# More unread products on TensorE, one ring slot more and one fewer, and fewer pooled sums on VectorE

## The chip, the cores and the metric

The kernel runs on one core of a Trainium2 chip. The metric is the time of one execution on the device, in microseconds. A core has five engines that run their own instruction queues in order: TensorE (PE in the profile; its weight loads are PEld), VectorE (DVE), ScalarE (ACT), GpSimd (POOL) and SyncE (SP), which issues most of the transfers.

## The reference

Three stages in a chain, all in float32, for 4 batches of 576 tokens:

```python
# 1 attention, 8 heads of 64: pooled by 4, plus a local window
q_d, k_d, v_d = (a.reshape(B, H, S // 4, 4, D).mean(axis=3) for a in (q, k, v))
x = np.repeat(sm_attn(q_d, k_d, v_d), 4, axis=2)        # softmax attention over 144 keys
x = x + local_attn(q, k, v)                             # keys with |i - j| < 4
# 2 experts: 8 of them, 512 -> 1024 -> 512, one per token
fresh_e = argmax(x @ w_gate)
e = fresh_e if s == 0 or sigmoid(x @ w_local) < 0.5 else prev_e   # prev_e of token s - 1
x = p[e] * (relu(x @ w1[e]) @ w2[e])                    # p: softmax of the gate
# 3 mixer
u = x + (relu(x.T @ w_tok1) @ w_tok2).T                 # over 576 tokens, hidden 256
out = u + relu(u @ w_ch1) @ w_ch2                       # 512 -> 1536 -> 512
```

## The kernel before

The work is split over a few classes. `Attn` does the attention and the routing, batch by batch. `Early` computes two of the experts, 256 rows each, for tokens of the first three batches, still inside the attention program. `Lead` fetches the first weights and rows of the rest. `Moe` then runs all experts by rank, and its `overflow` is a loop, with a length known only at run time, over surplus rows. `Mix` is the mixer. A float32 product is done as three products of high and low parts (the names wh, wl and c2h, c2l are such parts).

Three recorded programs follow one another: attention with `Early` and `Lead`, then `Moe`, then `Mix`. Class `Sched` records each operation with an estimated duration, and `Sched.order` puts the operations of a program into one order by simulating the engines, the buffers and priorities; line 527, 529 or 531 is where recorded operations are issued, so nearly all rows of the profile carry these lines. Each engine then executes its own operations in that order, and an operation that waits holds up everything behind it on its engine.

Buffers are rings. In attention `kz` (5 slots) holds the keys of a pair of heads, `vw` (NVW = 4 slots) values, `raw` (NRAW = 3 slots) loads that POOL sums up; a slot has 4 KB or more per partition. `Early` takes its weights through the same rings: `raw` for what SP loads, `kz` for the high parts and `vw` for the low parts.

Keys are pooled by four in `pool_k`, for each batch b, pair of heads pr (0 to 2) and half u, either by one sum on VectorE or by three additions on POOL:

```python
if (b, u) in KDVE:
    i("dve", "tensor_reduce", out=kd, in_=kv, axis=AX.X, op=ALU.add)
else:
    for k in range(1, 4):
        i("pool", "tensor_tensor", out=kd, in0=kd if k > 1 else kv[:, :, :, 0], in1=kv[:, :, :, k], op=ALU.add)
```

KDVE lists five pairs (b, u), so 15 of the 24 sums are on VectorE. Values of the batches 1 to 3 are pooled by POOL (`vd`, from `raw`). POOL also divides the local softmax (`p`) and builds masks for routing (`r_dg`).

`Sched.warm` adds products that nobody reads (lhsT `onesb`, rhs `rb`, 128x248, bf16; "unread products" below). After the planning it walks along TensorE's planned times, and where a planned gap has room it adds one, as long as the planned busy time of the last WINDOW = 3.4 us is below a share of it:

```python
used = sum(max(0.0, min(e, t) - max(b, t - WINDOW)) for b, e in done[-60:])
if cold or used < share * WINDOW:
    new.append((t, fn))
```

In the attention program (line 1694) the share is WARM = 0.5; in `Mix` (line 1667) MIX_WARM = (10.0, 0.5), that is the first 10 planned us with a share of 0.5. `Moe` has none. Between the programs of `Moe` and `Mix` stands the loop of `overflow`: line 1459 reads its length, and at line 1460 all engines meet before it (rows of semaphores at that line). Behind it, `Mix` begins with gathers on POOL (`x_f<-yd,pos`), then PE's transposes `x_t` of the rows.

Of the kernel before, what the change touches and what calls it, by code (L numbers as in the profile page):

```python
# [219 lines left out]
class Sched:  # L220
# [80 lines left out]
    def i(self, e, m, after=(), **kw):  # L301
        outs = [kw[k] for k in ("out", "accum_out") if kw.get(k) is not None]
        ins = [v for k, v in kw.items() if k not in ("out", "accum_out") and isinstance(v, (bass.AP, View))]
        acc = [(region(a), True) for a in outs] + [(region(a), False) for a in ins]
        c = self.cost(e, m, outs[0], ins, kw)
        if self.cur is not None:
            o = self.ops[self.cur]
            assert o["e"] == e
            o["calls"].append((m, kw))
            o["d"] += c  # L310
        else:
            self.ops.append(dict(e=e, calls=[(m, kw)], d=c, pred={}, use=[], init=None, stage=self.stage + self.shift, moves=True))
        k = len(self.ops) - 1
        o = self.ops[k]
        for p in after:
            o["pred"].setdefault(p, 0)
        for a in outs + ins:
            if isinstance(a, View) and a.buf not in o["use"]:
                o["use"].append(a.buf)
                a.buf.users.append(k)  # L320
        self.note(k, acc)
        return k
# [211 lines left out]
class Attn:  # L534
# [108 lines left out]
    def pool_k(self, b, pr):  # L643
# [5 lines left out]
        for u in range(2):  # L649
            r = slice(64 * u, 64 * u + 64)  # L650
            kv = kz[r, u, :, 3:195].rearrange("p h (g r) -> p h g r", r=4)
            kd = s["kd"][r, :, 48 * pr:48 * pr + 48]
            if (b, u) in KDVE:
                i("dve", "tensor_reduce", out=kd, in_=kv, axis=AX.X, op=ALU.add)
# [266 lines left out]
    def run(self, early):  # L921
        S_ = self.S
        do = lambda name, b, *args: S_.late((name, b), getattr(self, name), b, *args)
        do("load_q", 0)
        self.load_consts()
        for b in range(B):
            t0 = STEP * 3 * b
            S_.stage = t0 - D_LEAD * STEP if b else D0
            if b:
                do("load_q", b)  # L930
            for pr in range(3):
                do("load_u", b, pr)
                do("pool_k", b, pr)
                if pr:
                    do("pool_v", b, pr - 1)
            for hp in range(HP):
                do("pool_q", b, hp)
                do("d1", b, hp)
                do("d2", b, hp)
            for pr in range(3):  # L940
                S_.stage = t0 + STEP * pr
                do("l1", b, pr)
                do("l2", b, pr)
                for n in ((0,), (1, 2), (3, 4))[pr]:
                    do("x1", b, n)
            S_.stage = t0 + 3 * STEP + R_LAG * STEP
            if b == B - 1:
                stage, S_.stage = S_.stage, t0 + E_LAG * STEP
                S_.late("take", self.early.take)
                S_.stage = stage  # L950
            elif b == B - 2:
                S_.stage = t0 + 3 * STEP + E_LAG * STEP
            do("route", b)
            if b == B - 3:
                self.early = early()
# [142 lines left out]
def convert(S_, src, n, hi, lo, after=(), cf="cf", cs="cs", queue="dma"):  # L1098

    i = S_.i  # L1100
    raw = S_.next("cr")
    if src.dtype == mybir.dt.int64:
        i(queue, "dma_start", after=after, out=raw[:, 0:2 * n], in_=src.bitcast(I32))
        rv = raw[:, 0:2 * n].rearrange("p (n t) -> p n t", t=2)
        low, high = rv[:, :, 0], rv[:, :, 1]
        f = S_.next(cf, I32)[:, 0:n]
        i("dve", "tensor_scalar", out=f, in0=high, scalar1=3, scalar2=0x3FFFFFF8, op0=ALU.logical_shift_left, op1=ALU.bitwise_and)
        i("dve", "scalar_tensor_tensor", out=f, in0=low, scalar=29, in1=f, op0=ALU.logical_shift_right, op1=ALU.bitwise_or)
        i("dve", "scalar_tensor_tensor", out=f, in0=high, scalar=-0x40000000, in1=f, op0=ALU.bitwise_and, op1=ALU.bitwise_or)
        sq = S_.next(cs, F32)[:, 0:n]  # L1110
        i("act", "activation", out=sq, in_=high.bitcast(F32), func=AF.Square)
        f = f.bitcast(F32)
        i("pool", "tensor_single_scalar", out=sq, in_=sq, scalar=FLOOR, op=ALU.is_ge)
        i("pool", "tensor_tensor", out=f, in0=f, in1=sq, op=ALU.mult)
    else:
        f = raw.bitcast(F32)[:, 0:n]
        i(queue, "dma_start", after=after, out=f, in_=src)
    i("act", "copy", out=hi, in_=f)
    i("dve", "tensor_tensor", out=lo, in0=f, in1=hi.bitcast(F32), op=ALU.subtract)
# [252 lines left out]
class Moe(Experts):  # L1372
# [54 lines left out]
    def run(self):  # L1427
        NW = KF * NE
        prev, done = None, []
        t0 = 0.0  # L1430
        for n in range(NW):
            r, fb = divmod(n, KF)
            self.S.stage = t0
            t0 += 4 * (12 * CAPS[r] / 2400 + TILES[r] * 0.65)
            if n >= NLEAD:
                self.loadw(n)
            if fb == 3 and r + 1 < NE:
                self.gather(r + 1)
            h = self.mm1(r, fb)
            if prev is not None:  # L1440
                self.mm2(*prev)
            prev = (r, fb, h)
            done.append(len(self.S.ops) - 1)
            if n == 24:
                self.S.stage = t0
                self.zeros()
            if n >= 8 and n % CONV == 0 and self.jobs:
                self.S.stage = t0 + 60
                convert(self.S, *self.jobs.pop(0), after=(done[n - 6],))
        self.mm2(*prev)  # L1450
        assert not self.jobs
        self.S.issue(self.S.order(busy=dict(pe=PE_LATE)))

    def overflow(self):
        tc, nc = self.tc, self.nc
# [44 lines left out]
class Mix:  # L1500
# [147 lines left out]
    def run(self):  # L1648
# [18 lines left out]
        filler = lambda: self.nc.tensor.matmul(cold, at.onesb, at.rb, start=True, stop=True)  # L1667
        self.S.issue(self.S.warm(self.S.order(), filler, 0.107, MIX_WARM[0], MIX_WARM[1]))

# [46 lines left out]
            Mix(a, tc, at, rt, yd, out, c1t, c2, c2t, wtt).run()  # L1716


WARM, WINDOW = 0.5, 3.4
NKZ, NVW, NRAW = 5, 4, 3  # L1720
VPE = (0,)
KDVE = ((0, 0), (0, 1), (1, 0), (2, 0), (3, 0))
STEP, D_LEAD, R_LAG = 12.0, 1.0, 1.5
SLACK = 0.02
PE_LATE = 2.0
NLEAD, CONV, C2_EARLY = 1, 2, 4
RAW, RING = 3, 4
RING_F, TOK_FB = 26, 3
MIX_WARM = 10.0, 0.5
MARK = 1, 0  # L1730
SHIFT = {('d1', 0): -8, ('pool_qk', 0): 5, ('load_q', 0): -5, ('x1', 3): 14, ('load_u', 0): 1, ('load_v', 2): 9, ('route', 2): -8, ('load_u', 3): -9, ('d1', 1): 15, ('load_q', 1): 4, ('pool_qk', 3): 10, ('route', 3): 4, ('x1', 0): 5, ('l1', 3): -6, ('l1', 0): -5, ('d2', 2): -1, ('load_k', 3): -2, ('Lead', 'gather'): -8, ('Early', 'gather'): -23, ('load_v', 1): 2}
WARM0 = 0.0
# [23 lines left out]
```

## Time and profile before

| | us |
|---|---|
| median of three executions | 818.44 |
| lowest, highest | 816.65, 822.51 |
| profiled execution | 815.2 |
| its span in the trace | 813.4 |
| TensorE busy | 764.6 (94%) |
| TensorE weight loads | 635.8 (78%) |
| VectorE busy | 464.5 (57%) |
| ScalarE busy | 331.1 (41%) |
| GpSimd busy | 231.5 (28%) |
| mean granted TensorE clock | 0.987 |

Attention with the early experts lasts until about 214 us, the experts until 439 us, the mixer to the end. A share of busy time over the whole span mixes these three; the rows below go by stage. The profile names what ended an engine's idle time behind an arrow (`<-DVE sm` is an operation of VectorE that writes sm). A granted clock of 1.0 is 2.4 GHz on TensorE, 0.50 is 1.2 GHz.

### The profile page before, as it was taken

Reading aid. Unit: us, or ns where it says so; the run is one execution under the profiler, and the core shown is the slowest. Engines: PE = TensorE matmul, PEld = TensorE weight load, DVE = VectorE, ACT = ScalarE, POOL = GpSimd, SP = SyncE. Lnnn points to the kernel's source line nnn. Section 1 sums busy time; section 2 is a strip of 40 time slices with the busy share of each in tenths; the row PEclk is TensorE's granted clock in tenths of the full one; section 3 lists DMA queues with packets and bytes.
Section 4 is the critical chain, followed back from the end, with each engine's and each line's share of the span. In section 5 each row is a group of like instructions: output and inputs, shape, how many; then the busy total and the mean of one; then the engine's idle time right before and its main releaser. Section 6 shows DMA issues by size and latency. Waiting matters only on the chain. (4 is left out here: it accounts for less than half of the span.)

```text
span 813.4 us, 13914 instructions
## 1 busy us (share of the span) xinstructions
PE 764.6 (94%) x5318; PEld 635.8 (78%) x5318; DVE 464.5 (57%) x1025; ACT 331.1 (41%) x722; POOL 231.5 (28%) x191
## 2 busy tenths in 40 slices
PE   7898987978999998999896999999999999999998
PEld 4566774857898887888795887888888888888897
DVE  6688989696557878899952767531441144111121
ACT  1775867534435454666552534311321132110110
POOL 4676414450624546436401165200000000000000
PEclk9899999999999999999999999999999999999999
DMA  9986324636699866878664233002001200010010
GB/s 253 245 231 211 119 99 122 184 129 196 212 299 302 274 223 198 278 225 274 215 200 149 69 100 113 27 27 72 13 1 27 72 14 0 1 52 0 1 52 27
DMA packets 36346, 107.90 MB, mean 133 GB/s; under 512 B 5003, under 2 KB 5643, under 8 KB 35895
## 3 DMA queue, kind: packets, MB, share of 16 engines
q1 hardware_dynamic: 32359, 95.15, 37.2%
q0 software_dynamic: 3200, 10.28, 4.2%
q10 hardware_dynamic: 720, 1.57, 0.5%
q8 instruction: 42, 0.69, 0.3%
q14 instruction: 25, 0.20, 0.1%
HBM read 87.32 MB, written 19.66 MB: 132 GB/s over the span
## 5 line engine op out<-in xcount | busy, mean ns | idle before, releaser
L531 DVE SCALAR_TENSOR_TENSOR x_h<-x_m,x_h 128x512 fp32r<-128x512 f32 (+1 forms) x60 | 38.2, 637 | 194.9 <-ACT x_h L531 194.9
L527 PE MATMUL x_y<-x_h,c2h 128*128 128x512 f32 (+1 forms) x480 | 136.2, 369 | 0.0
L531 ACT ACTIVATE x_h<-x_m 128x512 fp32r<-128x512 f32 (+1 forms) x60 | 33.3, 554 | 201.1 <-PE x_m L527 176.1
L527 PEld LDWEIGHTS x_y<-x_h,c2h 128*128 128x128 f32 x480 | 86.6, 189 | 14.3
L527 PE MATMUL x_y<-x_h,c2l 128*128 128x512 f32 (+1 forms) x240 | 88.3, 368 | 0.0
L527 PE MATMUL y<-wh,h 128*128 128x512 f32 (+2 forms) x205 | 74.8, 402 | 1.8 <-DVE yo L531 1.2
L531 DVE TENSOR_TENSOR wl<-raw,wh 128x1024 fp32r<-128x1024 f32 (+1 forms) x47 | 59.9, 1277 | 18.4 <-ACT wh L531 18.0
L531 ACT CAST wh<-raw 128x1024 fp32r<-128x1024 f32 (+1 forms) x47 | 47.1, 1004 | 21.6 <-PE y L527 15.2
L531 POOL TENSOR_SCALAR cs<-cs 128x512 f32<-128x512 f32 (+1 forms) x21 | 38.1, 1812 | 49.8 <-ACT cs L531 49.1
L527 PEld LDWEIGHTS x_y<-x_h,c2l 128*128 128x128 f32 x240 | 45.2, 189 | 7.6
L527 PEld LDWEIGHTS y<-wh,h 128*128 128x128 f32 (+2 forms) x205 | 38.2, 188 | 12.1 <-DVE yo L531 2.5
L531 POOL TENSOR_TENSOR cf<-cf,cs 128x512 f32<-128x512 f32 (+1 forms) x21 | 39.6, 1884 | 27.9 <-DVE cf L531 26.3
L527 PE MATMUL y<-wl,h 128*128 128x512 f32 (+3 forms) x112 | 44.3, 395 | 0.0
L531 DVE SCALAR_TENSOR_TENSOR h<-m,h 128x256 fp32r<-128x256 f32 (+3 forms) x88 | 29.5, 358 | 8.5 <-ACT h L531 8.4
L531 ACT ACTIVATE h<-m 128x256 fp32r<-128x256 f32 (+6 forms) x64 | 25.4, 397 | 17.9 <-PE m L527 16.5
L531 DVE SCALAR_TENSOR_TENSOR cf<-cr,cf 128x512 int32<-128x512 int32 (+1 forms) x42 | 31.0, 739 | 0.7
L527 PE MATMUL m<-l_xh,wh 128*128 128x256 f32 (+2 forms) x96 | 29.2, 304 | 0.9 <-DVE h L531 0.9
L1126 POOL DMA_INDIRECT xg<-xd,q_xi x19 | 20.0, 1055 | 33.5 <-PE t L529 22.9
L527 PE MATMUL m<-l_xh,wl 128*128 128x256 f32 (+2 forms) x96 | 29.0, 302 | 0.2 <-DVE wl L531 0.2
L527 PE MATMUL m<-l_xl,wh 128*128 128x256 f32 (+2 forms) x96 | 28.8, 300 | 0.0
L531 ACT COPY pt<-pc 32x384 f32<-32x384 f32 x48 | 24.4, 509 | 10.7 <-DVE pc L531 10.0
L527 PE MATMUL y<-l_wh,h 128*128 128x512 f32 (+2 forms) x75 | 27.2, 402 | 1.1 <-DVE h L531 1.0
(810 smaller groups left out, 2035.8 us busy)
## 6 DMA issues: line engine op xcount, KB each, us to landing
raw<-in_wx SPq DMA_DIRECT2D x80, 512.0 KB
cr<-in_c SPq DMA_DIRECT2D x16, 512.0 KB
vw<-in_vw SPq DMA_DIRECT2D x12, 512.0 KB
kz<-in_kw SPq DMA_DIRECT2D x24, 200.0 KB
xd<-xn SPq DMA_DIRECT2D x16, 256.0 KB
yd<-zero SPq DMA_DIRECT2D x8, 512.0 KB
yd<-yo SPq DMA_DIRECT2D x15, 256.0 KB
x_cr<-in_c SPq DMA_DIRECT2D x7, 512.0 KB
```

The costliest lines, as they stand in the source:

```text
L527: f(kw.pop("out"), **kw)
L531: f(**kw)
L1126: nc.gpsimd.indirect_dma_start(out=t.real()[0:n, :], out_offset=None, in_=table, in_offset=bass.IndirectOffsetOnAxis(ap=index, axis=0))
```

## The change

```diff
@@ -1450,6 +1450,9 @@
         self.mm2(*prev)
         assert not self.jobs
         self.S.issue(self.S.order(busy=dict(pe=PE_LATE)))
+        at, cold = self.at, self.S.pools["t"][1][0][:, 264:512]
+        for _ in range(TAIL):
+            self.nc.tensor.matmul(cold, at.onesb, at.rb, start=True, stop=True)
 
     def overflow(self):
         tc, nc = self.tc, self.nc
@@ -1716,17 +1719,18 @@
             Mix(a, tc, at, rt, yd, out, c1t, c2, c2t, wtt).run()
 
 
-WARM, WINDOW = 0.5, 3.4
-NKZ, NVW, NRAW = 5, 4, 3
+WARM, WINDOW = 0.8, 3.4
+TAIL = 36
+NKZ, NVW, NRAW = 5, 5, 2
 VPE = (0,)
-KDVE = ((0, 0), (0, 1), (1, 0), (2, 0), (3, 0))
+KDVE = ((0, 0), (0, 1))
 STEP, D_LEAD, R_LAG = 12.0, 1.0, 1.5
 SLACK = 0.02
 PE_LATE = 2.0
 NLEAD, CONV, C2_EARLY = 1, 2, 4
 RAW, RING = 3, 4
 RING_F, TOK_FB = 26, 3
-MIX_WARM = 10.0, 0.5
+MIX_WARM = 14.0, 0.8
```

The two shares are raised to 0.8 and the mixer's first 10 us to 14. 36 unread products stand behind the last expert product and ahead of `overflow`. `vw` gets a fifth slot, `raw` loses its third. KDVE keeps two of its five pairs, so nine sums become 27 additions on POOL. As the planner works with these rings and engines, it also puts the whole attention program into another order; the orders of `Moe` and `Mix` change only by the unread products. Counted in the program, attention had 71 unread products (40 at its start, then groups of 15, 5, 2 and 9) and has 123: 59 at the start, then 22, 9, 2, 7, 9, 2 and 1 up to the first product of `Early`, and 2, 3 and 7 behind it. `Mix` had 19 (17 ahead of its first transposes) and has 30 (28 ahead of them). Lines behind the inserted three are shifted by 3, from the new constant on by 4.

On POOL, in attention, this is what stood from its third kd addition on (kd_116 is the pooled keys of batch 1, kz_89 and kz_90 slots of kz, vd_117 pooled values, raw_105 to raw_107 slots of raw); six kd additions were ahead of the first vd:

```order
L531 TENSOR_TENSOR kd_116<-kz_90 64x4x48
L531 TENSOR_TENSOR kd_116<-kd_116,kz_89 64x4x48
L531 TENSOR_TENSOR kd_116<-kd_116,kz_90 64x4x48 x2
L531 TENSOR_TENSOR vd_117<-raw_105 72x512
L531 TENSOR_TENSOR vd_117<-raw_106 72x512
L531 TENSOR_TENSOR kd_116<-kz_86 64x4x48
L531 TENSOR_TENSOR kd_116<-kd_116,kz_86 64x4x48
L531 TENSOR_TENSOR vd_117<-vd_117,raw_107 72x512
```

Now twelve kd additions are ahead of the first vd, and the piece begins with the last four of these (p_123 and p_124 are local softmax numerators, sm their reciprocal sums):

```order
L531 TENSOR_TENSOR kd_116<-kd_116,kz_89 64x4x48 x2
L531 TENSOR_TENSOR kd_116<-kd_116,kz_90 64x4x48 x2
L531 TENSOR_TENSOR vd_117<-raw_106 72x512
L531 TENSOR_TENSOR kd_116<-kz_86 64x4x48 x2
L531 TENSOR_TENSOR kd_116<-kd_116,kz_86 64x4x48 x4
L531 TENSOR_TENSOR p_124<-p_124,sm_135 128x512
L531 TENSOR_TENSOR p_123<-p_123,sm_136 128x512
L531 TENSOR_TENSOR vd_117<-raw_107 72x512
L531 TENSOR_TENSOR kd_115<-kz_87 64x4x48 x2
L531 TENSOR_TENSOR kd_115<-kz_88 64x4x48 x2
L531 TENSOR_TENSOR p_124<-p_124,sm_129 128x512
```

What moved: the additions for two slots of kz come in one piece, before any vd, and three divisions of p stand between the first vd and the third.

On PE, in the same program, where the rows of the early experts are transposed (xg are their gathered rows; pv products are local attention of the last batch, the products with wcat its gate logits; L1694 is an unread product), before:

```order
L1694 MATMUL m_150<-rb,onesb 128x248
L529 MATMUL g_153<-ca,xg_101 128x128 x4
L527 MATMUL pv_149<-pt_113,vw_93 64x96 x8
L527 MATMUL g_154<-wcat,xt_96 128x137 x2
L527 MATMUL g_151<-wcat,xt_96 128x137 x2
L529 MATMUL g_152<-ca,xg_102 128x128 x4
```

Now the products of the last batch stand in one piece ahead of these transposes, and unread ones between (L1697 is the same line as L1694; nine of them follow here):

```order
L527 MATMUL g_152<-wcat,xt_97 128x137 x2
L527 MATMUL g_153<-wcat,xt_97 128x137 x2
L527 MATMUL g_151<-wcat,xt_97 128x137 x2
L527 MATMUL g_154<-wcat,xt_97 128x137 x2
L529 MATMUL g_152<-ca,xg_102 128x128 x4
L1697 LDWEIGHTS onesb
L1697 MATMUL m_150<-rb,onesb 128x248
```

What moved: the transposes of the early experts' rows have gone behind the last batch's pv products, and unread products fill the places between them.

## Rows read from the trace of the kernel before

**Rows 1.** Engine busy time (and instructions), granted PE clock (PEclk), DMA share, by stage.
```profile
20.00:90.00 70.00, 61.47 (x863) 44.48 (x859) 53.90 (x135) 51.61 (x176) 47.78 (x53) 0.95 0.80 222
...
146.00:214.00 68.00, 59.87 (x414) 51.32 (x413) 48.20 (x160) 27.98 (x51) 23.79 (x16) 0.97 0.55 178
...
448.00:813.00 365.00, 360.95 (x1826) 304.62 (x1826) 127.54 (x255) 85.42 (x174) 40.95 (x33) 1.00 0.11 37
```

**Rows 2.** The same view: four stretches in which the granted clock was 0.50.
```profile
34.21:41.04 6.83, 6.83 (x42) 5.27 (x41) 3.49 (x8) 4.50 (x13) 5.91 (x7) 0.50 0.97 252
...
136.61:140.03 3.42, 3.39 (x13) 1.29 (x14) 3.00 (x10) 1.33 (x3) 1.40 (x2) 0.50 0.01 5
...
194.64:198.05 3.41, 3.41 (x17) 3.37 (x16) 0.75 (x3) 0.58 (x1) 0.00 (x0) 0.50 0.49 150
...
443.81:447.23 3.42, 2.97 (x15) 1.80 (x13) 0.00 (x0) 0.00 (x0) 2.66 (x3) 0.50 0.35 93
```

**Rows 3.** TensorE's timeline; start and length in us; in brackets idle time, releaser.
```profile
1.17 7.18 PE L1694 MATMUL m<-rb,onesb 128*128 128x248 bf16 x40 [1.17 <-DVE rb L525]
...
9.81 1.04 PE L527 MATMUL sl<-kz,qt 128*24 128x60 f32 x64 [1.25 <-DMA kz<-in_kw]
...
29.00 1.75 PE L1694 MATMUL m<-rb,onesb 128*128 128x248 bf16 x15
33.27 0.88 PE L527 MATMUL pv<-pt,vw 128*64 128x96 f32 x16 [2.52 <-ACT pt L531]
...
131.15 0.70 PE L1694 MATMUL m<-rb,onesb 128*128 128x248 bf16 x5
135.74 1.35 PE L527 MATMUL m<-r_ev,r_lh 128*128 128x144 f16 x5 [3.89 <-DVE r_ev L531]
```

**Rows 4.** Waits by engine and releaser, 20 to 90 us: sum, times, longest (us).
```profile
PE pv L527 <- ACT pt L531: 2.5, 1, 2.5
PE sl L527 <- DVE sm L531: 2.4, 1, 2.4
...
POOL vd L531 <- DMA raw<-in_vf: 5.8, 4, 2.9
POOL kd L531 <- DMA kz<-in_kw: 5.4, 4, 4.3
```

**Rows 5.** Line 1460, the loop's entry (ns min/median/max, first, last us), then TensorE's timeline.
```profile
L1460 PEldq EVENT_SEMAPHORE  x13: 51/51/51, 438.8 to 443.1; - x13
...
L1460 POOLq EVENT_SEMAPHORE  x12: 42/43/43, 405.1 to 443.0; - x12
...
443.42 3.36 PE L1667 MATMUL x_y<-rb,onesb 128*128 128x248 bf16 x17 [4.83 <-SPq L1460]
448.01 0.66 PE L529 MATMUL x_t<-ident,x_f 128*128 128x128 f32 x4 [1.23 <-DVE x_f L531]
```

**Rows 6.** Groups of instructions on kd: ns min/median/max, first and last start.
```profile
L531 POOL TENSOR_TENSOR kd<-kd,kz x18: 679/692/705, 24.3 to 87.7; 64x192 f32<-64x192 f32 x18
L531 DVE TENSOR_REDUCE kd<-kz x15: 903/935/952, 9.4 to 87.6; 64x192 f32<-64x768 f32 x15
```

**Rows 7.** Timelines: GpSimd's last kd sums, then TensorE's reading of them.
```profile
86.96 1.48 POOL L531 TENSOR_TENSOR kd<-kd,kz 64x192 f32<-64x192 f32 x2
...
105.14 0.95 PE L527 MATMUL g<-kd,qd 64*64 64x144 f32 x12
```

**Rows 8.** Timelines near 48 us: VectorE, then GpSimd.
```profile
47.91 1.16 DVE L531 TENSOR_SCALAR sm<-sm 128x16 f32<-128x16 f32 x1
...
47.76 1.27 POOL L531 TENSOR_TENSOR vd<-vd,raw 72x512 f32<-72x512 f32 x1 [2.88 <-DMA raw<-in_vf]
```

**Rows 9.** Early experts: SyncE's queue 150 to 206 us, TensorE's waits 146 to 214.
```profile
172.29 33.98 SPq L1157 DMA_DIRECT2D raw<-in_wx  x12
...
PE sl L527 <- DVE pd3x L531: 3.8, 2, 2.3
...
PE sl L527 <- ACT xg L531: 2.5, 1, 2.5
```

## Prediction

> **What bounds the kernel now.** I read four views. First the busy time of each engine by stage: from 20 to 90 us, where three batches of attention overlap, TensorE (PE) works 61.47 of 70 us, VectorE (DVE) 53.90, ScalarE 51.61 and GpSimd (POOL) 47.78, and the mixer from 448 us on is PE alone, 360.95 of 365 [rows 1]. So time is to be won in the front part only, and what is lost ahead of 448 us is not won back behind it. Second, the stretches in which the granted clock stood at 0.50, the lower of TensorE's two levels, 1.2 instead of 2.4 GHz: in three of the four shown PE was busy practically throughout, in the fourth it had only unread products to run [rows 2, 5]. Third, PE's timeline ahead of them: each follows a wait, such as 2.52 us ending at 33.27 and 3.89 us ending at 135.74 [rows 3]. In front of these waits the old kernel already puts unread products, 15 and 5 of them; in the first case they are over by 29.00 + 1.75 = 30.75 while PE waits until 33.27. Fourth, the lists of waits: in 20 to 90 us PE's largest ones are for ScalarE's pt (2.5 us) and DVE's sm (2.4 us), and POOL waits 5.8 + 5.4 = 11.2 us for transfers [rows 4]. What a change here is worth is therefore a matter of single waits of 1 to 4 us and of half-clock stretches of 3.4 us, out of 815.
>
> **The price of one unread product.** Fifteen of them in a row take 1.75 us and five take 0.70 [rows 3]; ten more cost 1.05, so 0.105 us each at full clock. The planner's own figure in the code is 0.107, which I use. Seventeen at half clock took 3.36 us [rows 5], about 0.2 us each.
>
> **The change, term by term**, against the profiled execution of 815.2 us; the median of the three runs is 818.4, 3.2 higher, and I carry the differences over to the median.
>
> *Start.* 59 unread products instead of 40. Forty take from 1.17 us on 7.18 us, until 8.35 [rows 3]; 19 more at 0.107 us take 2.0, until 10.4, so that the first kz product, which started at 9.81 after a wait of 1.25 us for its transfer [rows 3], follows near 10.5. That is 0.7 us late, of which the next waits may swallow a part. I take +0.3 (0 to +0.7).
>
> *The two clock falls in attention.* At 29.00 us now 22 instead of 15 products: 7 x 0.107 = 0.75 us more, and the 2.52 us wait shrinks to about 1.8. In the second place 11 instead of 5 (and one behind), so about 0.6 us of 3.89. If the clock then stays up, the first stretch (6.83 us with PE busy for 6.83) gives back half, 3.4 us, and the second (3.42 us, PE busy 3.39) 1.7 [rows 2]. Neither wait goes away, so I take half of 5.1: -2.5 (0 to -5.1).
>
> *DVE loses nine sums.* By the row of the fifteen sums one takes 0.935 us [rows 6]; nine in 20 to 90 us make 8.4 us off DVE's 53.90. What PE sees of it is at most its direct wait for DVE, 2.4 us for sm [rows 4]; most of DVE's other time is beside PE's work. -1.5 (0 to -2.4).
>
> *POOL gets them.* Each becomes three additions of 0.692 us [rows 6]: 27 x 0.692 = 18.7 us, which lifts POOL from 47.8 to 66.5 of 70 us. The cover is slack: for the last batch, POOL's last kd sum is done by 86.96 + 1.48 = 88.44 us and PE reads it at 105.14 [rows 7], 16.7 us later. But POOL's queue is in order, and in the new one twelve kd additions stand ahead of the first vd, where six stood, and later softmax divisions (p) come behind them. If POOL's waits for raw and kz, 5.8 and 5.4 us [rows 4], all remained beside 66.5 us of work, it would end at 77.7, 7.7 us too late. The waits shrink where POOL comes later to data that has landed, so I stay near the lower end: +1 (0 to +7.7).
>
> On the hold of POOL against DVE: a DVE operation on 16 numbers that began at 47.91 us lasted 1.16 us and ended within 0.05 us of a POOL addition of 1.27 us that ran from 47.76 [rows 8]. So a POOL addition can hold up a DVE operation for its whole length. The Trainium skill ("SBUF — State Buffer", "SBUF: two separate sides") says that the two engines share a port pair, that the first to start keeps it for its whole instruction and the other stands still; the trace agrees with these two rows. By that rule alone each of the 27 new additions could cost DVE up to 0.69 us, 18.7 us in all, more than the 8.4 us it is relieved of.
>
> *The other unread products.* Of the 52 new ones in the attention program 19 and 7 are told above; 26 remain, spread over the second fall and the early experts. Where the planner saw a gap that isn't there, each costs 0.107 us, 2.8 us in all; I take a quarter, +0.7 (0 to +2.8).
>
> *The early experts and the rings.* From 146 to 214 us PE is busy 59.87 of 68 us [rows 1]. Its waits are 3.8 us for DVE's pd3x and 2.5 us for ScalarE's xg [rows 9], and the stretch from 194.64 us at half clock [rows 2] costs 1.7. The weights come in through raw; SP issued twelve of these loads from 172.29 to 206.27 [rows 9], one each 33.98/12 = 2.8 us. In the new order the early experts begin when the last batch's local products are nearly over, with less interleaving and with the register reads of the expert earlier. That could remove the waits (-6.3) and the clock fall (-1.7), together -8.0. Against this stands raw with two slots instead of three: a load can be issued only when a slot is free, and if that sets the pace, the two pieces that lay ahead are lost, 2 x 2.8 = +5.7. The fifth vw slot, which holds the lower weights, works the other way. Between -8.0 and +5.7 I take -2.
>
> *The 36 products ahead of the surplus loop.* 36 x 0.107 = 3.85 us, so PE ends at about 438.8 + 3.85 = 442.6 instead of at 438.8, where its first semaphore of line 1460 stands [rows 5]. All engines meet there, and POOL's own last semaphore is at 443.0. So PE comes to the meeting just in time. Its thirteen semaphores took until 443.1 only because others were late; 13 x 0.051 us and as much again between them is 1.3 us, so its first mixer products would start near 444.4 instead of 443.42. There 28 unread products now stand where 17 stood: at full clock they end at 447.4, ahead of the first transposes at 448.01, at half clock (0.2 us each) at 450.0. No gain is possible at this place: the half-clock stretch from 443.81 to 447.23 held nothing but unread products [rows 2, 5], and the clock was up when real work began. I take +0.6 (0 to +2.0).
>
> Sum: 0.3 - 2.5 - 1.5 + 1 + 0.7 - 2 + 0.6 = -3.4, from the median 818.4 to **815.0 us**.
>
> **The rivals.**
> *A, a few us faster (the forecast):* single waits shrink, part of the clock comes back, 811 to 817. For it: the new products stand in front of waits that are in the trace. Against: none of the waits goes away.
> *B, nothing that can be told:* the planner's gaps are not the chip's, the unread products neither hold the clock nor cost anything, and the new order of the queues gives and takes at random, 817 to 820. For it: in the old kernel the 15 products at 29.00 stood just ahead of a fall, and did not prevent it.
> *C, the whole of it:* both falls in attention gone (-5.1), DVE's wait gone (-2.4), the early experts fed without stalls (-8.0), less the 0.3, 1, 0.7 and 0.6 that are paid: -12.9, 805.5. For it: all three sit in the same front part and one late wait feeds the next. Against: it needs every bound at once.
> *D, slower, POOL becomes the bound:* with 66.5 us of work in 70 its slack is 3.5 us. Once more than that remains of the 11.2 us in which it waits for raw and kz, vd, p and the masks of routing come late, and PE's pv products wait behind p. At the full 11.2 that is +7.7; with the two thirds of it +5.7 beside a lost gain. Place: 20 to 90 us. It gives 822 to 826, and each addition that holds up a DVE operation adds to it. Two raw slots, which feed vd as well, make it likelier. Against: kd has 16.7 us of slack in the last batch.
>
> **How the numbers follow.** A 0.48, B 0.20, C 0.15, D 0.17. The time of A is 815.0. A and B cover 811 to 820; to leave out no more than two in ten the range takes in the nearer half of C and of D: 806 to 823. About 1%, 8 us, is what a measurement of this kernel can tell from no change (three runs of it differ by 5.9 us). Faster by over 1% is below 810.3: all of C and a tenth of A, 0.20. Slower by over 1% is above 826.6: the upper third of D, 0.05. The rest, 0.75, is no change by that bound.
>
> **What would show it.** In the new trace: at the wait near 33 us the granted clock stays 1.0 behind it or it falls again; DVE's busy time in 20 to 90 us is near 45.5 us if POOL does not hold it, near 54 if it does; POOL's is near 66 us, and its waits for raw and kz are below 4 us (A) or near 11 (D). PE's wait for sm is shorter. In the early experts the list of waits shows pd3x and xg smaller, or waits for raw in their place. At the surplus loop PE's first semaphore is near 442.6 and the first transposes are within 1 us of where they were, counted from the last expert product. The forecast is wrong if the start of the mixer moves by more than 8 us either way, or if the mixer itself takes other than 365 us.

## Result and the profile after

The changed kernel takes 830.24 us (median of four runs, 829.18 to 833.02), the kernel before 819.5 in the same comparison; the ratio is 1.0136, with a 95% interval from 1.009 to 1.0182. It is slower by about 11 us where 3.4 us less was forecast. The profiled execution of the changed kernel is the longest of its four (833.0 us, span 831.2), that of before is shorter than its median (815.2, span 813.4). So the two traces differ by 17.8 us, and a part of that is chance.

By the starts of the same products in both traces the 17.8 us divide as follows. "Last pv" is the start of the last local attention product, "experts" the start of the first product of the stage behind the early experts (its weights are named l_wh), "last y" that of the last product with wh in that stage, "mixer" that of its first transposes.

| from, to | before, us | after, us | difference |
|---|---|---|---|
| start to last pv | 151.71 | 155.00 | +3.3 |
| last pv to experts (early experts) | 63.17 | 72.59 | +9.4 |
| experts to last y | 222.63 | 226.15 | +3.5 |
| last y to mixer | 10.50 | 11.38 | +0.9 |
| mixer to end of span | 365.4 | 366.1 | +0.7 |

Busy time by stage of the changed kernel (columns as in [rows 1]):

```profile
20.00:90.00 70.00, 63.35 (x861) 45.82 (x849) 47.62 (x129) 52.92 (x182) 56.74 (x72) 0.95 0.84 225
...
155.00:228.00 73.00, 61.87 (x391) 52.43 (x388) 49.78 (x152) 24.17 (x42) 18.52 (x14) 0.93 0.46 150
```

And the early experts of the kernel before, cut at its own last pv product:

```profile
152.00:215.50 63.50, 55.37 (x348) 47.70 (x349) 45.55 (x150) 23.44 (x42) 20.55 (x13) 0.97 0.55 175
```

In that stage PE stood idle for 73.00 - 61.87 = 11.1 us, before for 63.50 - 55.37 = 8.1. Its stretches at half clock, as in [rows 2]:

```profile
163.73:167.14 3.41, 3.40 (x17) 3.05 (x17) 2.98 (x10) 1.32 (x3) 0.00 (x0) 0.50 0.69 190
187.62:194.45 6.83, 4.80 (x18) 4.42 (x19) 5.07 (x25) 0.38 (x1) 0.00 (x0) 0.50 0.32 93
```

PE was busy in them for 3.40 + 4.80 = 8.2 us, of which half, 4.1, is lost; before it was 1.7 in one stretch. 31 unread products now lie in the stage (7, 9, 2, 1, 2, 3 and 7), 31 x 0.107 = 3.3 us, and none did before. That makes 3.0 of idle time, 2.4 of clock and 3.3 of unread products, 8.7 of the 9.5 us by which the two windows differ. The rest is about what eight more transposes of gathered rows (xg) take, which stood ahead of the last pv product before and stand behind it now (28 in the stage instead of 20; four take 0.60 us). The shares are not independent of each other: order_only, below, has none of the new unread products, and the stage takes 71.0 us in it.

The longest wait is this one, on PE's timeline:

```profile
183.66 0.40 PE L527 MATMUL sl<-vw1x,pd0x 128*128 128x512 f32 x1
189.65 0.80 PE L527 MATMUL sl<-kz1x,pd1x 128*128 128x512 f32 x1 [5.59 <-DVE pd1x L531]
```

PE waits for pd1x, an activation's low part that VectorE makes. VectorE's own timeline, and GpSimd's, tell what it did in that time:

```profile
178.66 0.21 DVE L531 TENSOR_REDUCE q_ex<-q_w 128x8 f32<-128x64 f32 x1
178.90 5.41 DVE L531 TENSOR_TENSOR q_w<-q_ohr,ca 128x64 f32<-128x64 f32 x1
...
189.18 0.41 DVE L531 SCALAR_TENSOR_TENSOR pd1x<-g,pd0x 128x256 fp32r<-128x256 f32 x1
...
178.48 0.96 POOL L1126 DMA_INDIRECT xg<-xd,q_xi  x1 [16.93 <-DVE pd1x L531]
179.46 2.41 POOL L531 TENSOR_TENSOR vw2x<-raw,kz2x 128x1024 fp32r<-128x1024 f32 x1
181.82 2.39 POOL L531 TENSOR_TENSOR vw3x<-raw,kz3x 128x1024 fp32r<-128x1024 f32 x1
```

A routing operation on 64 elements per partition (the next one of its form took 0.27 us) lasted from 178.90 to 184.31, and GpSimd's two subtractions of low weights, one right behind the other, ended at 184.21. When the routing operation began, 0.56 us ahead of the first of them, a gather of GpSimd was under way (178.48 to 179.44). Twenty-nine short routing operations stand behind it in VectorE's queue ahead of pd1x, so pd1x comes at 189.18 and PE has stood still since 184.06. From 187.62, still within the wait, the clock is at 0.50 until 194.45. The same kind of hold is in [rows 8], with 1.16 us; here it is nearly five times as long, in a place where VectorE's queue of routing is what PE waits for.

The stage's other stretch at half clock also follows a wait that lies behind a held operation of routing, beside the subtraction vw1x (159.20 to 161.55):

```profile
158.74 2.89 DVE L531 TENSOR_TENSOR r_lg<-lg 128x45 f32<-128x45 f32 x1
...
163.41 0.70 PE L527 MATMUL g<-r_dg,utri 128*128 128x256 f16 x2 [2.11 <-ACT xn L531]
```

The kernel before has the hold too. Beside three subtractions in a row, three short operations took 2.31, 1.70 and 1.90 us ahead of pd3x, which came at 170.95; this is the longer of PE's two waits for pd3x in [rows 9] (GpSimd, then VectorE, then PE):

```profile
163.78 2.39 POOL L531 TENSOR_TENSOR vw0x<-raw,kz1x 128x1024 fp32r<-128x1024 f32 x1 [9.36 <-issue]
166.14 2.53 POOL L531 TENSOR_TENSOR vw2x<-raw,kz2x 128x1024 fp32r<-128x1024 f32 x1
168.63 2.38 POOL L531 TENSOR_TENSOR vw3x<-raw,kz3x 128x1024 fp32r<-128x1024 f32 x1
...
163.89 2.31 DVE L531 TENSOR_TENSOR pall<-pall,r_sm 128x5 f32<-128x5 f32 x1
...
166.99 1.70 DVE L531 SCALAR_TENSOR_TENSOR q_key<-base,ca 128x8 f32<-128x8 f32 x1
...
169.14 1.90 DVE L531 CAST q_ki<-q_so 128x8 int32<-128x8 f32 x1
...
171.42 0.50 PE L527 MATMUL sl<-kz0x,pd3x 128*128 128x512 f32 x1 [2.29 <-DVE pd3x L531]
```

So the hold is not new; what would be new is how long PE stands still behind it. This reading of two traces is what the experiments test.

### The profile page after: what moved, and what is told of

The parts are those of the page before. It is cut to its first block, busy times and chain, and to the rows that moved or that the text cites. A ratio compares the mean times of both kernels' runs of the same rounds, so it can differ in the third digit from the quotient of the medians.

```text
span 831.2 us, 14134 instructions
## 1 busy us (share of the span) xinstructions
PE 779.3 (94%) x5417; PEld 648.0 (78%) x5417; DVE 465.9 (56%) x1016; ACT 330.7 (40%) x722; POOL 248.2 (30%) x218
## 5 line engine op out<-in xcount | busy, mean ns | idle before, releaser
L531 ACT ACTIVATE h<-m 128x256 fp32r<-128x256 f32 (+6 forms) x64 | 25.4, 397 | 17.8 <-PE m L527 12.7
L527 PE MATMUL pv<-pt,vw 128*64 128x96 f32 x384 | 23.1, 268 | 6.5 <-DVE xt L531 3.8
```

The source lines that it names most:

```text
L527: f(kw.pop("out"), **kw)
L531: f(**kw)
```

## Experiments

Code is shown in part; "..." marks a cut. All ratios are to the kernel before on the same chip, with 95% intervals. "Changed" is the kernel of the diff.

| kernel | ratio | interval |
|---|---|---|
| changed | 1.0136 | 1.009 to 1.0182 |
| fillers_only | 0.9968 | 0.9941 to 0.9995 |
| order_only | 1.0105 | 1.0065 to 1.0145 |
| kdve_only | 1.0110 | 1.0068 to 1.0152 |
| rings_only | 1.0028 | 0.9998 to 1.0059 |
| sums_moved_in_old_order | 1.0064 | 1.003 to 1.0098 |
| sums_back_in_new_order | 1.0143 | 1.0085 to 1.0201 |
| two_lows_on_dve | 1.0095 | 1.0066 to 1.0123 |
| all_lows_on_dve | 1.0034 | 1.0003 to 1.0066 |
| all_lows_and_sums_on_dve | 0.9998 | 0.9963 to 1.0033 |
| lows_on_dve_hold_kept | 1.0197 | 1.0158 to 1.0235 |
| fillers_lows_dve | 1.0007 | 0.9977 to 1.0038 |
| fillers_all_sums_on_dve | 1.0095 | 1.006 to 1.0131 |
| before_planned_lows | 0.9958 | 0.9925 to 0.999 |
| fillers_planned_lows | 0.9941 | 0.9908 to 0.9973 |
| changed_planned_lows | 0.9996 | 0.9967 to 1.0025 |

### Which part of the change

**The unread products alone, fillers_only.**

```diff
-NKZ, NVW, NRAW = 5, 5, 2
+NKZ, NVW, NRAW = 5, 4, 3
-KDVE = ((0, 0), (0, 1))
+KDVE = ((0, 0), (0, 1), (1, 0), (2, 0), (3, 0))
```

(taken from the changed kernel, so that the products stay)

> The kernel before, in its old order, with the new unread products alone: shares 0.8 and 0.8, the mixer's first 14 us, and the 36 ahead of the surplus loop. Theory 1 (the loss sits in the new order: in the early experts of the changed kernel a VectorE operation of 0.2 us lasted 5.41 us beside two GpSimd subtractions of 2.4 us, PE waited 5.59 us for it, and the clock fell behind it): within 3 us of before, that is -2 to +3 us, about +1 for the 36 products. Theory 2 (the unread products stand in the way of real work and cost their length, 52 x 0.107 = 5.6 us in attention, and about 1 us at the loop): +5 to +9 us.

0.9968: they gain about 2.6 us, a little more than theory 1 allowed. In this trace neither the fall of the clock near 34 us nor that near 195 us occurs any more; in attention and the early experts the lower level stands at 138.44 to 141.86 and 172.58 to 175.99 us. Theory 2 falls.

**All but the unread products, order_only.**

```diff
-WARM, WINDOW = 0.8, 3.4
-TAIL = 36
+WARM, WINDOW = 0.5, 3.4
+TAIL = 0
-MIX_WARM = 14.0, 0.8
+MIX_WARM = 10.0, 0.5
```

> The changed kernel without any of the new unread products: old shares, old 10 us, none ahead of the loop; rings, KDVE and with them the new order stay. Theory 1: +8 to +11 us over before, with a VectorE operation of over 4 us beside two GpSimd subtractions vw2x and vw3x in the early experts. Theory 2: -2 to +3 us.

1.0105, and the held operation is there again, with the same length:

```profile
181.37 5.41 DVE L531 TENSOR_TENSOR q_w<-q_ohr,ca 128x64 f32<-128x64 f32 x1
...
181.93 2.40 POOL L531 TENSOR_TENSOR vw2x<-raw,kz2x 128x1024 fp32r<-128x1024 f32 x1
184.29 2.40 POOL L531 TENSOR_TENSOR vw3x<-raw,kz3x 128x1024 fp32r<-128x1024 f32 x1
```

So the loss sits in what rings and KDVE bring, with the order that follows from them.

**KDVE alone and the rings alone**, each from the kernel before:

```diff
-KDVE = ((0, 0), (0, 1), (1, 0), (2, 0), (3, 0))
+KDVE = ((0, 0), (0, 1))
```

> The kernel before with KDVE cut to two pairs alone (nine sums become 27 additions on GpSimd; rings as before; the planner makes an order of its own). Theory 1a (the two raw slots are what packs the early experts' subtractions and loads together): -3 to +3 us. Theory 1b (GpSimd's longer queue makes routing and the last batch late): +5 to +11 us, with the last pv product later than 151.7 us by that much.

```diff
-NKZ, NVW, NRAW = 5, 4, 3
+NKZ, NVW, NRAW = 5, 5, 2
```

> The kernel before with five vw slots and two raw slots alone. Theory 1a: +6 to +11 us, all of it between the last pv product and the first product of the expert stage (63 us before, 70 or more here), with waits of ScalarE for raw. Theory 1b: -3 to +3 us.

1.0110 and 1.0028. Theory 1a, that two raw slots are what packs the early experts, falls: the rings cost little, about 2 us, with an interval that just reaches none. KDVE alone brings the loss, but only half of it where theory 1b had it. Its last pv product came at 156.95 (5.2 us later), and the stage behind it took 68.6 us instead of 63.2 (5.4 more), again with a wait of PE of 5.10 us for pd1x, and these rows on VectorE and GpSimd ahead of it:

```profile
174.25 2.45 DVE L531 TENSOR_TENSOR tab<-tab,r_tb 128x144 f32<-128x144 f32 x1
176.62 2.30 DVE L531 TENSOR_TENSOR q_nb<-q_nb,ca 128x8 f32<-128x8 f32 x1
...
174.11 2.42 POOL L531 TENSOR_TENSOR vw0x<-raw,kz1x 128x1024 fp32r<-128x1024 f32 x1 [14.46 <-PE sl L527]
176.50 2.40 POOL L531 TENSOR_TENSOR vw1x<-raw,kz2x 128x1024 fp32r<-128x1024 f32 x1
```

### GpSimd's sums, or the order

**Nine sums moved in the old order.** The plan is made as before; then the nine operations of (1, 0), (2, 0) and (3, 0), listed in MOVED, change their engine at their places.

```diff
...
+for n, kd, kv in MOVED:
+    at.S.ops[n]["e"] = "pool"
+    at.S.ops[n]["calls"] = [("tensor_tensor", dict(out=kd, in0=kd if k > 1 else kv[:, :, :, 0], in1=kv[:, :, :, k], op=ALU.add))
+                            for k in range(1, 4)]
```

> The kernel before in its old order, with the nine sums turned into three GpSimd additions each at the place that VectorE's sum had in the plan; nothing else changes, no new unread products. KDVE alone cost 10 us in an order of its own. Theory D (direct: GpSimd's longer queue and its holding of VectorE): +5 to +11 us over before, and VectorE's excess over its shortest durations grows from 16 us to 22 or more. Theory O (the new order that the planner makes of it packs routing and the early experts badly): -3 to +3 us.

1.0064, about 5 us: theory D holds in the old order, at the lower end of its range. In the trace the last pv product comes 7.2 us later than before (158.96), and the stage behind it is no longer than before (61.8 us). PE's longest wait in the first 90 us is there (PE, then VectorE, then GpSimd):

```profile
49.96 1.39 PE L527 MATMUL pv<-pt,vw 128*64 128x96 f32 x14 [5.58 <-DVE xt L531]
...
48.75 0.71 DVE L531 STREAM_TRANSPOSE pc<-p 128x512 f32<-128x512 f32 x1 [6.20 <-POOL p L531]
...
42.48 0.69 POOL L531 TENSOR_TENSOR kd<-kz 64x192 f32<-64x192 f32 x1
43.25 1.43 POOL L531 TENSOR_TENSOR kd<-kd,kz 64x192 f32<-64x192 f32 x2
44.76 1.45 POOL L531 TENSOR_TENSOR kd<-kz 64x192 f32<-64x192 f32 x2
46.29 1.43 POOL L531 TENSOR_TENSOR kd<-kd,kz 64x192 f32<-64x192 f32 x2
47.68 2.05 POOL L531 TENSOR_TENSOR p<-p,sm 128x512 f32<-128x512 f32 x2
```

The division p stands behind seven kd additions, VectorE waits 6.20 us for it, and the pv products need what is made from it. But the second half of the expectation failed. VectorE's excess (the time by which its operations in attention and the early experts exceeded the shortest of the same form and names, where by over 0.1 us) stayed at 16.7 us (15.8 before). So it is not more holding that costs here; GpSimd's longer queue is what the rows point to.

**The same nine sums back on VectorE, in the new order**, each in place of its three additions (ns).

```diff
...
+for ns, kd, kv in MOVED:
+    for n in ns:
+        at.S.ops[n]["calls"] = []
+    at.S.ops[ns[-1]]["e"] = "dve"
+    at.S.ops[ns[-1]]["calls"] = [("tensor_reduce", dict(out=kd, in_=kv, axis=AX.X, op=ALU.add))]
```

> The changed kernel in its new order, unread products and rings as changed, with the nine sums back on VectorE at the place that GpSimd's last addition had in the plan. Theory D: -3 to +3 us against before. Theory O: +6 to +11 us, with the VectorE operation of 5.4 us beside vw2x and vw3x still there and PE's wait of over 5 us for pd1x.

1.0143: nothing comes back. In the changed kernel the sums on GpSimd are thus not what costs; the order is, as theory O said. In this run PE waits 5.33 us for pd1x, and the held q_w takes 5.12 us.

### GpSimd's subtractions of low weights

**Two of them on VectorE**, in the changed kernel, the two beside the held operation (lows are GpSimd's six subtractions into vw, in the order of the plan); the order is kept.

```diff
...
+for k in lows[4:6]:
+    at.S.ops[k]["e"] = "dve"
```

> The changed kernel in its order, but the two subtractions vw2x and vw3x that GpSimd did one behind the other in the early experts, while VectorE's q_w stood still for 5.41 us, are done by VectorE at the same places in the plan (about 1.28 us each). If that hold is what makes PE wait 5.59 us and lets the clock fall behind it: 4 to 8 us less than the changed kernel, so +2 to +7 us over before, and PE's wait for pd1x there below 3.5 us. If the wait has another cause behind it (VectorE's routing work in front of pd1x as such): within 2 us of the changed kernel, +9 to +12.

1.0095: about 3.4 us of 11 come back (the intervals of this and of the changed kernel overlap). With 7.8 us over before it falls between the two ranges that were expected. The trace shows the expected step: the wait is 2.60 instead of 5.59 us,

```profile
186.40 0.50 PE L527 MATMUL sl<-kz1x,pd1x 128*128 128x512 f32 x1 [2.60 <-DVE pd1x L531]
```

the stretch at half clock behind it is 187.56 to 190.97 instead of 187.62 to 194.45, and the stage takes 67.9 us instead of 72.6.

**All six on VectorE**, the same edit without the index.

> The changed kernel in its new order, with all six subtractions of low weights of the early experts that GpSimd did put on VectorE at the same places in the plan. With two of them moved it was 0.95% over before instead of 1.36%. If GpSimd's holding of VectorE is the rest of the loss as well (the four others held it for 2.1, 2.05 and 2.75 us in routing): 0 to +3 us against before. If the rest is the order itself (who waits for whom in routing and in the last batch): +6 to +9 us.

1.0034. Of the changed kernel's 1.36% one per cent is gone, though VectorE now does six more operations of 1.2 us. In the two profiles the early experts are 7.2 us shorter than in the changed kernel (65.4 instead of 72.6), and the last pv product comes 3.4 us earlier. Three of the six stand ahead of it in the changed kernel, beside held operations of up to 2.39 us. VectorE's excess, as counted above, is 17.9 us, in the changed kernel 24.0. The rest of the new order costs at most little.

**All six, and the sums back too.**

> The same, and the nine sums also back on VectorE at the places of the new order, so that GpSimd does no more than before in any stage. If the extra work on GpSimd is the rest of the loss: -3 to +2 us against before. If the order itself is: +5 to +9 us, about the same as with the six subtractions alone.

0.9998. By the two ratios the extra additions on GpSimd cost 0.3% once the larger loss is gone; the intervals overlap, so that they cost anything there is not shown.

**The hold without the dependence.** Moving the subtractions does two things: VectorE is not held, and the weights no longer come from GpSimd. This run keeps them apart: VectorE makes the weights, and GpSimd does the same subtraction besides, into a buffer that nobody reads.

```diff
...
+def both(kw=kw):
+    r = {n: v.real() if isinstance(v, View) else v for n, v in kw.items()}
+    nc.vector.tensor_tensor(**r)
+    nc.gpsimd.tensor_tensor(**dict(r, out=scratch))
+at.S.ops[k]["calls"] = [(both, None)]
```

> The changed kernel with the six subtractions done by VectorE at the same places, and each of them also done by GpSimd at its old place into a buffer that nobody reads, so that GpSimd is as busy and can hold VectorE as in the changed kernel, but no product waits for GpSimd's result. With the six moved and GpSimd free it was 0.34% over before. If holding VectorE is the cause of the loss: +8 to +13 us against before, with single VectorE operations of 2.2 to 5.4 us again. If what counted was that the weights came late from GpSimd: 0 to +5 us.

1.0197, against 1.0034 without the useless subtractions: 1.6%, some 13 us, for six operations whose result nobody reads. With 16 us over before it is more than the 8 to 13 expected if the hold is the cause, and far from the 0 to 5 expected if late weights are. The held operations are back (first two rows VectorE, last two GpSimd):

```profile
180.70 3.09 DVE L531 TENSOR_TENSOR q_inc<-q_ex,q_ov 128x8 f32<-128x8 f32 x1
...
184.97 2.39 DVE L531 TENSOR_TENSOR q_w<-q_ohr,ca 128x64 f32<-128x64 f32 x1
...
181.33 2.42 POOL L1702 TENSOR_TENSOR scratch<-raw,kz2x 128x1024 fp32r<-128x1024 f32 x1
183.83 3.45 POOL L1702 TENSOR_TENSOR scratch<-raw,kz3x 128x1024 fp32r<-128x1024 f32 x1
```

GpSimd stands still too: its second subtraction took 3.45 us instead of 2.4, beside VectorE's own vw2x (183.84 to 185.05). VectorE thus has the subtractions to do here and is held besides, which is more than it has in the changed kernel; the kernel to compare with is the one with GpSimd free. PE's waits from 150 to 231 us, first of this kernel, then of that one:

```profile
PE sl L527 <- DVE pd1x L531: 7.1, 2, 6.5
PE g L527 <- ACT xn L531: 3.8, 1, 3.8
...
```

```profile
PE sl L527 <- DVE pd1x L531: 3.6, 3, 2.6
...
PE g L527 <- ACT xn L531: 0.4, 1, 0.4
...
```

Two things are not separated. GpSimd's reading also keeps a slot of raw until it is done, so a load can start later. ScalarE's waits for raw from 130 to 230 us are 12.4 us in this kernel and 10.5 with GpSimd free, a small part of the difference; PE does not wait for raw in either. And GpSimd's later gathers stand behind the useless subtractions; this kernel's list has no wait of PE for them.

### Versions that might beat both

**The old order with the unread products and all six lows on VectorE in place**, the edit of all_lows_on_dve on fillers_only.

> A candidate: the kernel before with the new unread products alone (3 us faster than before when it ran), and all six subtractions of low weights of the early experts that GpSimd did put on VectorE at the same places. If GpSimd's holding of VectorE costs the old order time as well (two of 2.3 us there): 2 to 5 us faster than with the unread products alone, so -5 to -8 us against before. If VectorE, whose queue is in order, now waits itself for the loads of these weights in the middle of routing: 0 to +6 us against before.

1.0007: no gain over the unread products alone. In place, VectorE is rid of the longest holds (its excess falls from 16.3 to 10.3 us), but it has to do the work in the middle of a plan that was not made for it; that this is what takes the gain back is argued, not shown.

**The old order with all nine other sums on VectorE too**, the edit of sums_back_in_new_order on fillers_only, for u = 1.

> A candidate and the converse of moving sums to GpSimd: the kernel before in its old order with the new unread products, and the nine sums that GpSimd did (27 additions) moved to VectorE in place. Moving nine the other way in the old order cost 5 us. If that price is GpSimd's time and its hold: -5 to -8 us against before. If VectorE is what is short there (53.90 of 70 us busy, 62 then): 0 to +5 us.

1.0095, so about 10 us lost against fillers_only, and more over before than either range expected. Moving sums from one engine to the other in place costs either way. Where it costs here is not shown: the profiled execution is the fastest of the ten (820.61 us; the median is 827.0), and PE's waits for VectorE's sm and lg in 20 to 90 us, 4.0 and 2.5 us, are about those of fillers_only (4.5 and 2.4).

**Lows planned on VectorE**: one word in the class of the early experts, ahead of the planning, with the unread products, then with the whole change, then with nothing else.

```diff
-    LO, CUT, QUEUE = "pool", 1, "act"
+    LO, CUT, QUEUE = "dve", 1, "act"
```

> A candidate in which the planner knows of it: the kernel before with the new unread products, the low weights of the early experts put on VectorE ahead of the planning, so that the order is made for it. If the hold is what counts: -3 to -8 us against before, with no VectorE operation held for over 2 us in routing. If any new order costs what the planner does not see: +2 to +10 us.

> The whole change, with the low weights of the early experts put on VectorE ahead of the planning. If the hold is the cause and KDVE and the rings cost little without it: -4 to +2 us against before. If KDVE's additions on GpSimd cost 5 us in any order, as they did in the old one: +3 to +8 us.

> The kernel before, without any part of the change, with the low weights of the early experts on VectorE ahead of the planning; with the new unread products besides it was 0.59% faster than before. If the unread products are worth the 0.3% that they brought in the old order: -1 to -4 us against before. If all of the gain came from the products' order and VectorE: -4 to -7 us.

0.9941, 0.9996 and 0.9958. The first is the best version: 815.93 us, about 5 us faster than before. In it the stage from the last pv product to the experts takes 57.8 us instead of 63.2, and PE works nearly without a pause:

```profile
152.50:210.35 57.85, 54.99 (x366) 46.48 (x360) 46.66 (x157) 23.40 (x42) 9.86 (x8) 1.00 0.59 196
```

With nothing else 0.4% are gained, so most of it comes with the subtractions and the order that the planner makes for them, which no run separates; the share of the unread products, 0.2%, lies within the intervals. The whole change on top of it is as fast as before and no faster. That is in the first of the two ranges expected, but not for its reason: against the first version KDVE and rings cost nearly 0.6%, about the 5 us of the second.

## Why the prediction was wrong

**The step that failed** is the term "the early experts and the rings", taken at -2 us between -8.0 and +5.7. The stage took 9.4 us longer in the trace, outside both bounds. The upper bound was built from loads (two slots of raw, 2 x 2.8 us); rings_only shows that the rings cost about 2 us in all. What fills the term is GpSimd's hold of VectorE during the subtractions of low weights: with all six on VectorE the loss falls from 1.36% to 0.34%, and with GpSimd doing them besides, for nothing, it is 1.97%. The hold itself was in the prediction, with a row and a rule, but was costed only for the 27 new additions of 0.69 us in 20 to 90 us. The operations of 2.4 us in the early experts, which exist in both kernels, were not counted, since the change does not touch them. It moves them: in the new order a routing operation stands through two of them in a row, and PE waits 5.59 us for a low part that VectorE makes behind it and some thirty small operations. Part of the hold was already in the term without its name. It counted PE's 3.8 us for pd3x as a wait that a new order could remove; 2.29 of these stand behind three operations held for 2.31, 1.70 and 1.90 us.

**The rule that was weighed then.** The Trainium skill ("SBUF — State Buffer", "SBUF: two separate sides") says that of GpSimd and a VectorE operation that has two SBUF inputs or runs in a two-port mode, the one that starts first keeps the shared ports for its whole instruction and the other stands still. The trace agrees that VectorE was held: 5.41 us where an operation of the same form took 0.27. It stood through two instructions of GpSimd, so one instruction is no bound on what a held operation costs. By the records it began 0.56 us before the first of the two, so which of them was first is not settled by these rows.

**Start, +0.3.** 59 products end at 10.27 us and the first kz product starts at 10.73, 0.9 us later than before ([rows 3]); what of it reached the end is not separable.

**The falls of the clock, -2.5.** This term failed too, in its sign. Its mechanism held at the first place: the wait shrank from 2.52 to 1.56 us and the clock stayed up behind it, and so it did in fillers_only. But the changed kernel has other waits, and the lower level at 20.37 to 23.78, at 85.22 to 88.64 and, in one piece, at 136.42 to 146.66 us instead. PE is busy in these for 15.2 us, of which half, 7.6, is lost, against 5.1 before: +2.5 where -2.5 was forecast. A part of that belongs to this execution; its mean granted clock, 0.978, is the lowest of the four (the others have 0.981 to 0.985).

```profile
32.48 2.49 PE L1697 MATMUL m<-rb,onesb 128*128 128x248 bf16 x22
36.53 0.88 PE L527 MATMUL pv<-pt,vw 128*64 128x96 f32 x16 [1.56 <-ACT pt L531]
...
20.37:23.78 3.41, 3.41 (x19) 1.78 (x18) 0.69 (x1) 0.34 (x2) 0.44 (x1) 0.50 1.04 236
85.22:88.64 3.42, 3.28 (x10) 1.95 (x10) 1.81 (x8) 0.94 (x3) 3.08 (x6) 0.50 0.47 163
136.42:146.66 10.24, 8.52 (x72) 6.09 (x71) 8.58 (x29) 3.99 (x7) 3.54 (x3) 0.50 0.33 103
```

**VectorE -1.5, GpSimd +1.** VectorE's busy time in 20 to 90 us fell by 6.3 us instead of 8.4, GpSimd's rose to 56.7, not to 66.5, since other work left the window (its kd additions there rose from 27 to 51, by 16.1 us). The signs of the busy times were right. The price of the two terms together was too low for the old order, where it was about +5 us (sums_moved_in_old_order); in the new one, once the hold was gone, the runs do not tell it from none. GpSimd's waits for raw and kz shrank to 1.7 and 3.7 us, as forecast; a wait of p for sm took their place:

```profile
POOL p L531 <- DVE sm L531: 13.6, 3, 11.4
POOL kd L531 <- DMA kz<-in_kw: 3.7, 2, 3.4
POOL vd L531 <- DMA raw<-in_vf: 1.7, 2, 1.5
```

**The other unread products, +0.7.** All unread products together gained 0.32% in the old order. In the new one, changed against order_only, they gained nothing that can be told.

**The 36 products, +0.6.** 10.50 us became 11.38 between the same products, +0.9; in fillers_only it is 10.01. The difference is the clock: PE waits about 2.1 us for the loop in both, and in the changed kernel the clock is at half behind that wait, from 460.69 to 464.10, in fillers_only it is not. On PE's timeline, after and then fillers_only:

```profile
460.73 4.55 PE L1670 MATMUL x_y<-rb,onesb 128*128 128x248 bf16 x26 [2.08 <-issue]
465.12 0.60 PE L529 MATMUL x_t<-ident,x_f 128*128 128x128 f32 x4
```

```profile
446.21 2.92 PE L1670 MATMUL x_y<-rb,onesb 128*128 128x248 bf16 x26 [2.12 <-issue]
449.20 0.66 PE L529 MATMUL x_t<-ident,x_f 128*128 128x128 f32 x4
```

So the term was right in its range, and that no gain lies there was nearly right too: half a microsecond, in the good case.

**The rivals.** D came closest: slower, with GpSimd's hold in it. Its place (20 to 90 us), its operations (the additions) and its bound (GpSimd) were wrong, and with 0.17 it had too little. The sentence that single waits of 1 to 4 us are at stake was near: the largest piece is one of 5.6 us and the clock behind it. The prediction's own sign of being wrong came: the start of the mixer moved by 17.1 us (448.01 to 465.12), while the mixer took 366 us.

Two of the smaller workings do not come out, and neither enters the sum: two thirds of 7.7 us are 5.1 and not 5.7, and the tails taken from A (a tenth below 810.3) and from D (the upper third above 826.6) lie outside the 811 to 817 and 822 to 826 that these were given.

**What stays open.** The stage of the experts, 3.5 us longer in the profiled execution, has the same order in both kernels. Between the same marks it took 222.7 us in the profile of kdve_only, 223.9 in two_lows_on_dve and 226.0 in sums_back_in_new_order, so the difference does not go with the loss; what makes it vary, no run here tells. What places the operations in the new order so badly is not traced to a rule of the planner; only that its costs know of no hold is plain from the code.

## What to carry to other kernels

When a change lets a planner order a program anew, the forecast has to take in what the change does not touch: list the long operations of the engine that can hold another one, and see beside which short operations they come to stand and who waits behind these. Work that GpSimd does beside VectorE was not free here, where VectorE is on the way to TensorE: in the changed order six subtractions of 2.4 us cost 8 us, and one word that moved them to VectorE ahead of planning gained 0.4% where the whole change lost 1.4%. Moved in place, in the old order, they gained nothing. To tell a hold from a late result, let both engines do the work and throw one result away.

## What the hardware showed unexpectedly

A VectorE operation that is held by GpSimd does not always get in between two GpSimd operations that follow one another: it stood 5.41 us through two of 2.4 us in the changed kernel and in order_only, and 5.12 us in sums_back_in_new_order. In order_only another stood 3.26 us beside three of together 3.71 us:

```profile
49.22 3.26 DVE L531 TENSOR_SCALAR sm<-sm 128x3 f32<-128x3 f32 x1
...
48.74 3.71 POOL L531 TENSOR_TENSOR vd<-vd,raw 72x512 f32<-72x512 f32 x3
```

In kdve_only VectorE did get in after one, for a single operation (2.45 us, then the next held for 2.30), and in the kernel before it did so beside three subtractions in a row (2.31, 1.70 and 1.90 us). In the three cases of over 5 us a gather of GpSimd was under way when the operation began, 0.3 to 0.6 us ahead of the first subtraction; in kdve_only and before, the first held operation began 0.1 us behind the start of the subtraction. A gather by itself did not hold such an operation: in the changed kernel one of the same form took 0.27 us from 184.62, within the gather of 184.37 to 185.33. What decides between the two, the runs do not show.
